# An adaLN attention and Mish block on one core: six weight slices split in the prologue, constant rows filled by GpSimd, loads respaced, and one TensorE visit for each modulation vector

## The chip, the cores and the metric

The kernel runs on one core of a Trainium2 chip. The time is what the device takes for one launch, in microseconds (us), taken as the median of several runs. The engines are TensorE (PE; its weight loads are PEld), VectorE (DVE), ScalarE (ACT), GpSimd (POOL) and SyncE (SP). All of the kernel's transfers are issued by SP, in one order, and run on the core's 16 DMA engines.

## The reference

A block of a transformer that is conditioned by a vector `c`, in float32, with 2048 rows of width 512, 32 heads of 16, and a hidden width of 1792:

```python
mod = (_silu(c) @ w_mod).reshape(c.shape[0], 6, 1, -1)
sa, ca, ga, sb, cb, gb = (mod[:, 0], mod[:, 1], mod[:, 2], mod[:, 3], mod[:, 4], mod[:, 5])
h = _layernorm(x, axis=-1) * (1 + ca) + sa
x = x + ga * _A_ref(h, A_wqkv, A_wo)          # softmax attention over all 2048 keys
h = _layernorm(x, axis=-1) * (1 + cb) + sb
x = x + gb * _B_ref(h, B_w1, B_b1, B_w2)      # (h @ w1 + b1) -> mish -> @ w2
```

The six modulation vectors are numbered 0 to 5 in this order, so `ga` is 2 and `gb` is 5.

## The kernel before

**Precision.** Products that must keep float32 accuracy are made from a high and a low part of each operand (`hi_copy`, L89, and `lo_sub`, L97): three products instead of one. Weights are split once and kept in DRAM as pairs (`w1scr`, `woscr`, `w2scr`).

**Steps.** Attention is worked in 32 turns `n`: a turn is four heads against one block of 512 queries, and has 16 steps `t`, so the main loop (`step`, L1227) has 512 steps. A step makes four 128x512 blocks of scores (L536), their exponentials on ACT (L539), the products with the values (`pv`, L554, once in a step), and, for the turn that comes 20 steps later, the row maxima of the scores (L487 on TensorE, L489 on VectorE). Scores, maxima and transposes share a ring of six PSUM banks. The maxima leave VectorE as a small tile `mt` (`max_rows`, L514), and SP writes it in four transfers of 4 KB into two extra rows of the query tiles `qa`, so that the score product subtracts the maximum itself. That put stands six half steps (three steps) before turn `n` starts, and must have landed by then.

**Work beside.** A score or maximum product uses 64 of TensorE's 128 rows. The other 64 rows take the remaining matrix products: the projections of q, k and v for later heads, the output product with `wo`, and the MLP. They wait in a list of units (`next_part`, L1185) that every two steps take up to eight products from, and small jobs stand in a list of specials (`do_specials`, L1330), which is visited after a step's products and goes to TensorE's queue between them and the step's `pv`.

**Order.** Nothing is scheduled by a compiler. The order is written out by hooks: `at(h, f)` runs `f` at half step `h = 2t`, and so places its instructions on the queue of each engine; a turn has 32 half steps. Half steps below 0 are the prologue, in which the maxima of turn 0 and part of turn 1 are made while the first projections run (`whole_units`, L1204). `store_at` (L193), `load_at` (L198) and `clear` (L189) move the stores and loads of the weight slices out of the half steps around the puts of `mt` (half step 26 of a turn). An engine's queue runs in order, so a hook's place does not tell its time: SP goes on as soon as the next transfer's buffer and data are free.

**Constant rows.** The key tiles `ka` and query tiles `qa` (five pairs in turn) have 64 rows for each of two heads: 48 rows of data, then rows of ones in `ka` and rows of zeros or of `mt` in `qa`. `zer` and `one` are 128x512 tiles; SP copies them into `qa` (`zeros`, L413) and into `ka` 0 and 1 (L419); `ka` 2 to 4 get their ones from `ka` 0 (L1428).

**Modulation.** Vectors 2 to 5 are each made in two halves: `mod_load` (L645) loads 512 KB of `w_mod`, three GpSimd operations multiply it by silu(c) and halve it twice (L652 to L654), and a special (`mod_unit`, L658) sums the 128 partitions on TensorE. For a gate (2 and 5) a half is one product of 256 columns, else two of one column.

**Weight slices.** 32 slices of 256 KB (14 of w1, 4 of wo, 14 of w2) are each loaded, split on GpSimd and stored as 512 KB (`prep_unit`, L678), one after the other by `start_preps` (L1392) from half step 60 on. Their tile `hl` has two buffers, later three. When all are stored and the projections are done, the memory of the projections becomes the MLP's (`prep_step`, L1403), and `first_loads` (L822) brings the first weights and rows of x.

```python
then = load_at(max(h + PREP, puts[0] + 1 if len(puts) > 2 - (not three) else 0))
at(then, lambda: start_preps(then, i + 1, turn + 1 if three else 0, puts))
```

Of the kernel before, what the change touches and what calls it, by code (L numbers as in the profile page):

```python
# [8 lines left out]
F32 = mybir.dt.float32  # L9
F32R = mybir.dt.float32r  # L10
# [8 lines left out]
def adaln_block(ctx: ExitStack, tc: tile.TileContext, x, wqkv, wo, w1, b1, w2, c, w_mod, out):  # L19
# [104 lines left out]
    def mm(acc, l, r, start, stop):  # L124
        pe_queue.append((acc, l, r, start, stop))
# [71 lines left out]

    def load_at(h):  # L198

        return h if h < 60 or 2 <= h % 32 < 20 else h - h % 32 + 28 if 20 <= h % 32 <= 28 else h + -(h - 2) % 32  # L200

    def at(h, f):

# [122 lines left out]
    with ExitStack() as es:  # L326
# [22 lines left out]
        slice_load(1, 1, pw)  # L349
        zer = lp.tile([P, TB], F32, name="zer")  # L350
        nc.gpsimd.memset(zer, 0.0)
        one = lp.tile([P, TB], F32, name="one")
        nc.gpsimd.memset(one, 1.0)

        e = lp.tile([P, DK], F32, name="sil_e")
        nc.scalar.activation(e, cc, AF.Exp, scale=-1.0)
# [53 lines left out]
        stats_tb(1)  # L410
        tr_tb(0)
        apply_tb(1)
        def zeros(i):  # L413
            for b in (48, 112):
                nc.sync.dma_start(qa[i][b:b + 16, :].bitcast(F32), zer[:16, :])

        for i in range(2):
            for b in (48, 112):
                nc.sync.dma_start(ka[i][b:b + 16, :].bitcast(F32), one[:64, :])  # L419
            zeros(i)  # L420

        def constants():
            for i in range(2, NR):
                zeros(i)
# [40 lines left out]

    kq2 = ctx.enter_context(tc.tile_pool(name="kq2", bufs=1))
    ka += [kq2.tile([P, S], F32R, name=f"ka{i}") for i in range(2, NR)]
    ap = ctx.enter_context(tc.tile_pool(name="ap", bufs=1, reuse_waits="tile"))
    vgs = {}

# [186 lines left out]

    def mod_unit(i):  # L658

        v, o = divmod(i, 2)  # L660
        gate = v in (2, 5)
        acc, row = ring(), mst.pop(("wm", i))[:, 0]
        if gate:
            mm(acc[:, :2 * P], ones.to_broadcast([P, P]), row, True, True)
        else:
            for m in range(2):
                mm(acc[:, m:m + 1], row[:, m * P:(m + 1) * P], ones, True, True)

        def fin(h):
            if gate:  # L670
                nc.scalar.copy(gates[(v - 2) // 3][:, o * 2 * P:(o + 1) * 2 * P], acc[:, :2 * P])
            elif v == 4:
                nc.vector.tensor_scalar_add(modc[:, v - 1, 2 * o:2 * o + 2], acc[:, :2], 1.0)
            else:
                nc.vector.tensor_copy(modc[:, v - 1, 2 * o:2 * o + 2], acc[:, :2])
        return fin

    def prep_unit(h, third, scr, src, gate):  # L678
# [113 lines left out]
    def block(qb, t0):  # L792
# [7 lines left out]
        def load(h, d, load_, keys):  # L800

            for j, k in enumerate(keys):
                at(h + 2 * j, lambda k=k: d.__setitem__(k, load_(k)))

        def more_w2(h, n):

            for j in range(n):
                k = mst["w2 at"]
                b, i = divmod(k, DK + FT)
                mst["w2 at"] += 1  # L810
                if b < NB - 1:
                    d, f, i = (state[b][3], load_wo, i) if i < DK else (state[b][2], load_w2, i - DK)
                    load(h + 2 * j, d, f, (i,))
                    if f is load_wo and i == DK - 1:
                        mst["wo at", b] = h + 2 * j
                elif i >= DK and i < DK + 3:
                    load(h + 2 * j, state[b][2], load_w2, (i - DK,))
                else:
                    mst["w2 at"] -= 1
                    break  # L820

        def first_loads(h):  # L822
            mst["w2 at"] = 0
            more_w2(h + 1, NA)
            load(h + 2, y, lambda i: load_y(qb, i), range(4))
            load(h + 9, w1s, load_w1, range(2))
            for i in range(4):
                mst["y at", qb, i] = h + 2 + 2 * i

# [529 lines left out]
        return fin  # L1359

    at(-2 * PRO, lambda: slice_load(*plan[2][1:3]))
    order = (4, 5, 10, 11, 6, 7, 8, 9)

    def first_mods(h):
        for i in order[:2]:
            mod_load(i, h)

    def queue_mod(j):
        def make():
            put = mod_unit(order[j])  # L1370

            def fin(h):
                put(h)
                if j + 2 < len(order):
                    mod_load(order[j + 2], h)
                elif j + 1 == len(order):
                    start_preps(h + 2)
            return fin

        queue_special(lambda: mst.get(("row at", order[j]), 4 * T) + 6, make)  # L1380

    for j in range(len(order)):
        queue_mod(j)
# [8 lines left out]
    def start_preps(h, i=0, turn=0, puts=()):  # L1392

        if i == len(preps):
            mst["open"] = (max(puts) + 2) // 2
            return
        three = (2, 1, NKC - 1) in put_away
        prep_unit(h, three and turn % 3 == 2, *preps[i])
        puts = (*puts, store_at(h + 9))[-3 if three else -2:]
        then = load_at(max(h + PREP, puts[0] + 1 if len(puts) > 2 - (not three) else 0))  # L1400
        at(then, lambda: start_preps(then, i + 1, turn + 1 if three else 0, puts))

    def prep_step(t):  # L1403
# [19 lines left out]
    at(2 * (T - 28), lambda: load_ys((0, 1)))  # L1423
    at(2 * (T - 12), lambda: load_ys((2,)))
    at(2 * T - 30, tail_loads)
    for pp in range(2, NR):
        for b in (48, 112):
            nc.sync.dma_start(ka[pp][b:b + 16, :].bitcast(F32), ka[0][b:b + 16, :].bitcast(F32))  # L1428
    for pp, h in ((2, -22), (3, -8)):
        at(h, lambda pp=pp: load_pair(pp))  # L1430
    def run_hooks(h):
# [39 lines left out]
```

## Time and profile before

| what | us |
|---|---|
| median of 3 runs (1700.04 to 1704.23) | 1703.48 |
| the profiled execution | 1704.48 |
| its span, first to last instruction | 1702.7 |
| start of the first `pv` (L554) | 109.7 |
| start of the last `pv` | 1600.8 |

The profile has a page of summaries; other views give single instructions in order of time (the timeline: start, duration, engine, line, what it writes and reads, how many, and in brackets the idle time before it with what ended it), the waits of each engine, and for chosen stretches the busy time of each engine, TensorE's granted clock (PEclk, 1.00 is full) and the share of time in which the 16 DMA engines were busy. A row of SP shows when a transfer is issued, not when it lands.

### The profile page before, as it was taken

What the parts mean: (1) busy time and instruction counts of PE and PEld (TensorE: products, weight loads), DVE (VectorE), ACT (ScalarE), POOL (GpSimd) and SP (SyncE); (2) the same over time, 40 slices, a digit from 0 to 9 for tenths busy, and PEclk for the clock granted to TensorE, in tenths of its full rate; (3) what the DMA queues carried; (4) which work ended last, traced back from release to release, by engine and by line L of the source; (5) the groups of instructions that cost most, each with busy time, mean ns of one, the idle gap of its engine ahead of it and who ended that gap; (6) DMA issues with size and microseconds to landing.
All of it is one profiled execution on the core that took longest, in us unless ns stands there. A gap on an engine that the chain in (4) does not pass through costs nothing.

```text
span 1702.7 us, 33730 instructions
## 1 busy us (share of the span) xinstructions
PE 1674.4 (98%) x12406; PEld 921.7 (54%) x12406; DVE 1438.2 (84%) x2372; ACT 1359.4 (80%) x2614; POOL 809.3 (48%) x829
## 2 busy tenths in 40 slices
PE   7999999999999999999999999999999999999999
PEld 5755665455444545555555455555555455555587
DVE  6888888888889898888889898888889888884377
ACT  6257777777778998888888998888888988888674
POOL 5155224565513465645433464655323564555442
PEclk9999999999999999999999999999999999999999
DMA  7777467777773343425364434435354433433261
GB/s 252 186 233 216 111 163 214 238 229 217 236 219 94 89 105 90 128 78 135 80 161 122 129 73 109 124 76 139 78 141 134 130 93 76 142 105 127 78 229 62
DMA packets 113997, 240.08 MB, mean 141 GB/s; under 512 B 24048, under 2 KB 49648, under 8 KB 107784
## 3 DMA queue, kind: packets, MB, share of 16 engines
q1 hardware_dynamic: 113832, 237.92, 49.5%
q8 instruction: 98, 1.61, 0.4%
q14 instruction: 67, 0.55, 0.1%
HBM read 179.95 MB, written 51.44 MB: 136 GB/s over the span
## 4 chain that ended last, share of the span: by engine, by line
PE 90%; DVE 3%; DMA 3%; ACT 2%; issue 1%; SPq 0%; POOL 0%; ACTq 0%; DVEq 0%; POOLq 0%
PE bk L554 28%; PE ring L536 22%; PE ring L487 19%; PE bk L136 10%; PE bk L129 3%; PE ring L1162 2%; PE ring L129 2%; DVE mx L489 2%; ACT pr L539 1%; DMA qa<-mt 1%; DMA xt<-in_A_x 1%; PE ring L501 1%; DMA w<-w1scr 1%; DMA w<-woscr 1%; PE ring L865 0%
## 5 line engine op out<-in xcount | busy, mean ns | idle before, releaser
L489 DVE TENSOR_REDUCE mx<-ring 128x1 f32<-128x512 f32 x1968 | 1222.9, 682 | 159.5 <-PE ring L487 138.0
L539 ACT ACTIVATE pr<-ring 128x512 f32<-128x512 f32 x2048 | 1079.0, 602 | 216.2 <-PE bk L136 118.0
L487 PE MATMUL ring<-ka,qa 64*128 64x512 f32 x1968 | 819.0, 429 | 3.0 <-DMA od<-ot 1.3
L536 PE MATMUL ring<-qa,ka 64*128 64x512 f32 x2048 | 761.3, 403 | 6.8 <-DMA qa<-mt 4.0
L554 PE MATMUL bk<-pr,vg 128*32 128x512 f32 x4096 | 546.8, 606 | 0.0
L487 PEld LDWEIGHTS ring<-ka,qa 64*128 64x128 f32 x1968 | 350.8, 184 | 331.6 <-DVE mx L489 248.1
L536 PEld LDWEIGHTS ring<-qa,ka 64*128 64x128 f32 x2048 | 374.1, 184 | 201.5 <-DVE mx L489 114.0
L136 PE MATMUL bk<-h,w 64*128 64x512 f32 (+1 forms) x1080 | 279.0, 391 | 0.0
L136 PE MATMUL bk<-w,a_h 64*128 64x512 f32 x632 | 210.6, 413 | 0.0
L136 PEld LDWEIGHTS bk<-h,w 64*128 64x128 f32 x1080 | 178.3, 184 | 9.6 <-ACT pr L539 1.5
L554 PEld LDWEIGHTS bk<-pr,vg 128*32 128x32 f32 x4096 | 80.8, 108 | 136.9 <-issue 127.8
L136 PE MATMUL bk<-w,a_l 64*128 64x512 f32 x316 | 124.2, 393 | 0.0
L136 PEld LDWEIGHTS bk<-w,a_h 64*128 64x128 f32 x632 | 106.9, 184 | 2.6
L921 POOL TENSOR_TENSOR y<-yd,y 128x512 f32<-128x512 f32 x44 | 56.9, 1293 | 89.5 <-ACT yd L920 84.6
L756 POOL TENSOR_SCALAR qq<-ee 128x512 f32<-128x512 f32 x25 | 15.5, 622 | 169.1 <-ACT ee L750 169.1
L772 POOL TENSOR_TENSOR qq<-qq,rr 128x512 f32<-128x512 f32 x42 | 54.2, 1291 | 83.6 <-ACT rr L766 83.4
L758 POOL TENSOR_TENSOR hb<-hb,ee 128x512 f32<-128x512 f32 x42 | 54.1, 1289 | 82.4 <-DVE ee L754 80.4
L136 PE MATMUL bk<-w,o_hl 64*128 64x512 f32 x288 | 79.8, 407 | 0.0
L98 POOL TENSOR_TENSOR a_l<-hb,a_h 128x512 fp32r<-128x512 f32 x53 | 72.2, 1363 | 4.4
L136 PEld LDWEIGHTS bk<-w,a_l 64*128 64x128 f32 x316 | 58.3, 184 | 2.3
L136 PE MATMUL bk<-h_h,wl 64*128 64x512 f32 x168 | 57.5, 423 | 0.0
L774 POOL TENSOR_TENSOR rr<-rr,qq 128x512 f32<-128x512 f32 x42 | 54.1, 1289 | 3.5
(206 smaller groups left out, 1857.9 us busy)
## 6 DMA issues: line engine op xcount, KB each, us to landing
ka<-kscr SPq DMA_DIRECT2D x124, 384.0 KB
w<-w2scr SPq DMA_DIRECT2D x56, 512.0 KB
w<-w1scr SPq DMA_DIRECT2D x46, 512.0 KB
vg<-vscr SPq DMA_DIRECT2D x32, 552.0 KB
qa<-qscr SPq DMA_DIRECT2D x124, 100.0 KB
kscr<-qh SPq DMA_DIRECT2D x16, 512.0 KB
qscr<-qh SPq DMA_DIRECT2D x32, 256.0 KB
hl<-in_B_w SPq DMA_DIRECT2D x28, 256.0 KB
```

Of the source, the lines that this page charges most:

```text
L98: (nc.gpsimd if eng == "p" else nc.vector).tensor_sub(lo, src, hi.bitcast(F32))
L129: nc.tensor.matmul(acc, l, r, start=start, stop=stop)
L136: i = nc.tensor.matmul(acc, l[64 * g:64 * g + 64], r[64 * g:64 * g + 64], start=start and not then, stop=bool(stop and then))
L487: nc.tensor.matmul(pm, qt[64 * s:64 * s + 64, qs * P:(qs + 1) * P], kt[64 * s:64 * s + 64, kb * TB:(kb + 1) * TB], start=True, stop=True)
L489: nc.vector.tensor_reduce(out=mxs[n][:, s, 4 * j + qs, kb:kb + 1], in_=pm, op=ALU.max, axis=AX.X)
L536: nc.tensor.matmul(p_, kt[64 * s:64 * s + 64, kc * P:(kc + 1) * P], qt[64 * s:64 * s + 64, :], start=True, stop=True)
L539: e = nc.scalar.activation(pr, p_, AF.Exp, scale=SCALE)
L554: nc.tensor.matmul(accs[n][32 * h:32 * h + 32, :], vgs[n][:, o:o + 32], pts.pop((t, h)), start=(kc == 0), stop=(kc == 15))
L758: (nc.vector if tail else nc.gpsimd).tensor_mul(hb, hb, ee)
L772: nc.gpsimd.tensor_mul(qq, qq, rr)
L774: nc.gpsimd.tensor_mul(rr, rr, qq)
L921: nc.gpsimd.tensor_add(y[i], yd, y[i])
```

## The change

```diff
-        return h if h < 60 or 2 <= h % 32 < 20 else h - h % 32 + 28 if 20 <= h % 32 <= 28 else h + -(h - 2) % 32
+        return h if h < 60 or 4 <= h % 32 < 20 else h - h % 32 + 28 if 20 <= h % 32 <= 28 else h + -(h - 4) % 32
...
-        one = lp.tile([P, TB], F32, name="one")
-        nc.gpsimd.memset(one, 1.0)
+        for i in range(NR):
+            nc.gpsimd.memset(qa[i].bitcast(F32), 0.0)
+        for i in range(2):
+            nc.gpsimd.memset(ka[i].bitcast(F32), 1.0)
...
-        def zeros(i):
-            for b in (48, 112):
-                nc.sync.dma_start(qa[i][b:b + 16, :].bitcast(F32), zer[:16, :])
-
-        for i in range(2):
-            for b in (48, 112):
-                nc.sync.dma_start(ka[i][b:b + 16, :].bitcast(F32), one[:64, :])
-            zeros(i)
...
+    for t in ka[2:]:
+        nc.gpsimd.memset(t.bitcast(F32), 1.0)
...
-    def mod_unit(i):
-
-        v, o = divmod(i, 2)
+    def mod_unit(v):
+
         gate = v in (2, 5)
-        acc, row = ring(), mst.pop(("wm", i))[:, 0]
-        if gate:
-            mm(acc[:, :2 * P], ones.to_broadcast([P, P]), row, True, True)
-        else:
-            for m in range(2):
-                mm(acc[:, m:m + 1], row[:, m * P:(m + 1) * P], ones, True, True)
+        acc, rows = ring(), [mst.pop(("wm", 2 * v + o))[:, 0] for o in range(2)]
+        for o, row in enumerate(rows):
+            if gate:
+                mm(acc[:, o * 2 * P:(o + 1) * 2 * P], ones.to_broadcast([P, P]), row, True, True)
+            else:
+                for m in range(2):
+                    mm(acc[:, 2 * o + m:2 * o + m + 1], row[:, m * P:(m + 1) * P], ones, True, True)
...
-            more_w2(h + 1, NA)
+            more_w2(h + 1, DK)
             load(h + 2, y, lambda i: load_y(qb, i), range(4))
-            load(h + 9, w1s, load_w1, range(2))
+            load(t0 + 7, w1s, load_w1, range(2))
+            at(t0 + 10, lambda: more_w2(t0 + 11, NA - DK))
...
-    order = (4, 5, 10, 11, 6, 7, 8, 9)
-
-    def first_mods(h):
-        for i in order[:2]:
-            mod_load(i, h)
+    order = (2, 5, 3, 4)
+
+    def first_mods(h, j=0):
+        for o in range(2):
+            mod_load(2 * order[j] + o, h + 2 * o)
...
+    EARLY = 6
+
+    def early_prep(i, h):
+
+        scr, src, _ = preps[i]
+        lo, hi = [ap.tile([P, TB], F32R, tag=f"p{(1, 3, 0, 2)[i % 4]}", name="ep", bufs=4 - i % 4 // 2) for _ in range(2)]
+        raw = lo.bitcast(F32)
+        nc.sync.dma_start(raw.rearrange("p (k m) -> p k m", m=P), src)
+
+        def split():
+            hi_copy("p", hi, raw)
+            lo_sub("p", lo, raw, hi)
+
+        def put():
+            for v, part in enumerate((hi, lo)):
+                nc.sync.dma_start(scr[:, v, :], part.bitcast(F32))
+
+        at(h + 7, split)
+        at(h + 10, put)
+
+    for i in range(EARLY):
+        at(3 * i - 34, lambda i=i: early_prep(i, 3 * i - 34))
...
-        then = load_at(max(h + PREP, puts[0] + 1 if len(puts) > 2 - (not three) else 0))
+        then = load_at(max(h + PREP, puts[0] + 2 if len(puts) > 2 - (not three) else 0))
...
-            at(32 * (n - 2) + (15 if n % 2 == 0 else 9), lambda n=n: load_pair(2 * n))
+            at(32 * (n - 2) + (2 if n in (3, 4, 5, 7) else 15 if n % 2 == 0 else 9), lambda n=n: load_pair(2 * n))
...
-    for pp in range(2, NR):
-        for b in (48, 112):
-            nc.sync.dma_start(ka[pp][b:b + 16, :].bitcast(F32), ka[0][b:b + 16, :].bitcast(F32))
```

The first six slices of w1 go through tiles of the exponentials' buffers during the prologue (`early_prep`), and `start_preps` begins with slice 6, at half step 66 instead of 60. The five `qa` and five `ka` tiles are filled whole by GpSimd. Both halves of a vector are loaded at one hook and their products stand in one special; the second half's three GpSimd operations come two half steps after the first's. The first pair of tiles of turns 3, 4, 5 and 7 is loaded 7 to 13 half steps earlier. Of the MLP's first loads, two slices of w1 and three of w2 come some 30 half steps later.

Three places on SP's queue show what moves. The first is the prologue, from the constants on; `ka` and `qa` with a number are the tiles of one pair, `wr` a raw slice of wqkv, `ep` a raw slice of w1, `vq` values on their way to DRAM. Before:

```order
L428 DMA b1c<-in_B_b 128x14x1
L1428 DMA ka_634<-ka_104 16x2048 x2
L1428 DMA ka_635<-ka_104 16x2048 x2
L1428 DMA ka_636<-ka_104 16x2048 x2
L231 DMA wr<-in_A_wqkv 128x4x128
L295 DMA vscr<-vq 128x4x272 x2
L310 DMA qa_108<-qscr 50x512 x2
L319 DMA ka_634<-kscr 48x2048 x2
```

and changed:

```order
L419 DMA b1c<-in_B_b 128x14x1
L231 DMA wr<-in_A_wqkv 128x4x128
L1393 DMA ep<-in_B_w 128x4x128 x2
L295 DMA vscr<-vq 128x4x272
L1393 DMA ep<-in_B_w 128x4x128 x2
L295 DMA vscr<-vq 128x4x272
L1401 DMA w1scr<-ep 128x512 x2
L1393 DMA ep<-in_B_w 128x4x128
L310 DMA qa_108<-qscr 50x512 x2
L319 DMA ka_625<-kscr 48x2048 x2
```

The six copies of ones are gone, and slice loads and their stores stand ahead of the next pair of tiles. The second place is the put of `mt` for turn 5 (`hl` is a slice, `rb` the reciprocal sums, `vg` the values). Before:

```order
L231 DMA wr<-in_A_wqkv 128x4x128
L689 DMA w1scr<-hl 128x1024
L682 DMA hl<-in_A_wo 128x512
L592 DMA rb<-rscr 64x1x512
L689 DMA woscr<-hl 128x1024
L474 DMA vg<-vscr 128x1104
L269 DMA qscr<-qh 8x16x512 x2
L269 DMA qscr<-ql 8x16x512
L525 DMA qa_106<-mt 2x4x128
```

and changed:

```order
L231 DMA wr<-in_A_wqkv 128x4x128
L675 DMA hl<-in_B_w 128x512
L682 DMA woscr<-hl 128x1024
L585 DMA rb<-rscr 64x1x512
L467 DMA vg<-vscr 128x1104
L269 DMA qscr<-qh 8x16x512 x2
L269 DMA qscr<-ql 8x16x512
L682 DMA woscr<-hl 128x1024
L518 DMA qa_106<-mt 2x4x128
```

The slice's load no longer stands behind the store just ahead of it, and one slice's store has moved from ahead of `vg` to right ahead of the four puts. The third place is the second pair of turn 9 (`qa_110`), behind the MLP's first loads (`y` are rows of x, `w` weight pairs). Before:

```order
L713 DMA y<-in_A_x 128x512
L695 DMA w_5841<-w2scr 128x1024
L695 DMA w_5843<-w1scr 128x1024
L695 DMA w_5869<-w2scr 128x1024
L695 DMA w_5871<-w1scr 128x1024
L310 DMA qa_110<-qscr 50x512 x2
L319 DMA ka_636<-kscr 48x2048 x2
```

and changed:

```order
L706 DMA y<-in_A_x 128x512
L688 DMA w_5833<-woscr 128x1024
L706 DMA y<-in_A_x 128x512
L310 DMA qa_110<-qscr 50x512 x2
L319 DMA ka_627<-kscr 48x2048 x2
```

Four slices of 512 KB that stood between the rows of x and the pair have gone from there; one slice and one row tile have come in their place.

More of the change, by code (lines that the diff above doesn't have):

```diff
@@ L412, in adaln_block @@
         apply_tb(1)
-        def zeros(i):
-            for b in (48, 112):
-                nc.sync.dma_start(qa[i][b:b + 16, :].bitcast(F32), zer[:16, :])
-        for i in range(2):
-            for b in (48, 112):
-                nc.sync.dma_start(ka[i][b:b + 16, :].bitcast(F32), one[:64, :])
-            zeros(i)
         def constants():
-            for i in range(2, NR):
-                zeros(i)
             for q4 in range(S // TB):
@@ L656, in mod_load @@
         at(h + 7, sums)
-    def mod_unit(i):
-        v, o = divmod(i, 2)
+    def mod_unit(v):
         gate = v in (2, 5)
-        acc, row = ring(), mst.pop(("wm", i))[:, 0]
-        if gate:
-            mm(acc[:, :2 * P], ones.to_broadcast([P, P]), row, True, True)
-        else:
-            for m in range(2):
-                mm(acc[:, m:m + 1], row[:, m * P:(m + 1) * P], ones, True, True)
+        acc, rows = ring(), [mst.pop(("wm", 2 * v + o))[:, 0] for o in range(2)]
[5 more added lines that the diff above has]
+                    mm(acc[:, 2 * o + m:2 * o + m + 1], row[:, m * P:(m + 1) * P], ones, True, True)
         def fin(h):
             if gate:
-                nc.scalar.copy(gates[(v - 2) // 3][:, o * 2 * P:(o + 1) * 2 * P], acc[:, :2 * P])
+                nc.scalar.copy(gates[(v - 2) // 3], acc)
             elif v == 4:
-                nc.vector.tensor_scalar_add(modc[:, v - 1, 2 * o:2 * o + 2], acc[:, :2], 1.0)
+                nc.vector.tensor_scalar_add(modc[:, v - 1, :], acc[:, :DK], 1.0)
             else:
-                nc.vector.tensor_copy(modc[:, v - 1, 2 * o:2 * o + 2], acc[:, :2])
+                nc.vector.tensor_copy(modc[:, v - 1, :], acc[:, :DK])
         return fin
@@ L1373, in fin @@
                 put(h)
-                if j + 2 < len(order):
-                    mod_load(order[j + 2], h)
-                elif j + 1 == len(order):
+                if j + 1 < len(order):
+                    first_mods(h, j + 1)
+                else:
                     start_preps(h + 2)
             return fin
-        queue_special(lambda: mst.get(("row at", order[j]), 4 * T) + 6, make)
+        queue_special(lambda: mst.get(("row at", 2 * order[j] + 1), 4 * T) + 6, make)
     for j in range(len(order)):
@@ L1390, in adaln_block, with start_preps @@
     preps += [(w2scr[f], w2[f * P:(f + 1) * P, :], 1) for f in range(FT)]
-    def start_preps(h, i=0, turn=0, puts=()):
+    EARLY = 6
[14 more added lines that the diff above has]
+        at(3 * i - 34, lambda i=i: early_prep(i, 3 * i - 34))
+    def start_preps(h, i=EARLY, turn=0, puts=()):
         if i == len(preps):
```

## Prediction, made before the changed kernel was run

> **What bounds the kernel now.** I read the page first: its busy times, the chain of waits, then the groups that the chain waits in.
>
> ```profile
> PE 1674.4 (98%) x12406; PEld 921.7 (54%) x12406; DVE 1438.2 (84%) x2372; ACT 1359.4 (80%) x2614; POOL 809.3 (48%) x829
> PE 90%; DVE 3%; DMA 3%; ACT 2%; issue 1%; SPq 0%; POOL 0%; ACTq 0%; DVEq 0%; POOLq 0%
> PE ring L536 <- DMA qa<-mt: 4.0, 3, 2.0
> PE ring L487 <- DMA od<-ot: 1.3, 1, 1.3
> ```
>
> PE is busy 98% of the span and 90% of the chain, so a transfer or a GpSimd operation counts only where PE waits for it. The view of waits (total, times, longest) has two such places in the main loop: three waits for the rows of `mt`, and one that it puts down to an output store. The timeline shows what they cost. A `pv` (L554) closes each step, so the distance of two `pv` is the step.
>
> ```profile
> 334.38 1.06 PE L554 MATMUL bk<-pr,vg 128*32 128x512 f32 x8
> 337.27 1.06 PE L554 MATMUL bk<-pr,vg 128*32 128x512 f32 x8
> 340.32 0.46 PE L536 MATMUL ring<-qa,ka 64*128 64x512 f32 x1 [1.98 <-DMA qa<-mt]
> 342.76 1.08 PE L554 MATMUL bk<-pr,vg 128*32 128x512 f32 x4
> ...
> 435.84 0.46 PE L536 MATMUL ring<-qa,ka 64*128 64x512 f32 x1 [1.76 <-DMA qa<-mt]
> ...
> 490.74 1.06 PE L554 MATMUL bk<-pr,vg 128*32 128x512 f32 x8
> 494.03 0.46 PE L487 MATMUL ring<-ka,qa 64*128 64x512 f32 x1 [1.26 <-DMA od<-ot]
> 496.12 1.94 PE L554 MATMUL bk<-pr,vg 128*32 128x512 f32 x8
> 500.04 1.06 PE L554 MATMUL bk<-pr,vg 128*32 128x512 f32 x8
> ```
>
> A step takes 337.27 - 334.38 = 2.89. The first step of turn 5 takes 342.76 - 337.27 = 5.49, and the two steps around 494 take 500.04 - 490.74 = 9.30 instead of 5.78: 3.52 lost for a gap of 1.26. The granted clock tells why (window, length, busy time of PE, PEld, DVE, ACT and POOL, PEclk, DMA share, GB/s):
>
> ```profile
> 341.00:346.00 5.00, 5.00 (x32) 2.29 (x29) 3.13 (x6) 2.60 (x6) 3.88 (x5) 0.66 0.94 190
> 494.00:498.00 4.00, 3.97 (x22) 1.57 (x22) 2.09 (x4) 1.77 (x3) 0.00 (x0) 0.62 0.06 11
> ```
>
> Behind both gaps the clock falls to 0.66 and 0.62 of full. At 0.66 over 5.00 us the loss is 0.34 x 5.00 = 1.70, so turn 5 costs about 1.98 + 1.60 = 3.58. For turn 7 I count the gap alone, 1.76.
>
> **What makes the puts late.** SP's rows and the DVE rows that make `mt`:
>
> ```profile
> 320.13 0.50 SPq L689 DMA_DIRECT2D w1scr<-hl  x1
> 327.86 0.33 SPq L682 DMA_DIRECT2D hl<-in_A_wo  x1
> 330.05 0.34 DVE L519 SCALAR_TENSOR_TENSOR mt<-mh,lows,ring 32x128 fp32r<-32x128 f32 x1 [0.42 <-ACT mh L518]
> 332.85 2.76 SPq L525 DMA_DIRECT2D qa<-mt  x4
> ...
> 379.68 0.34 DVE L519 SCALAR_TENSOR_TENSOR mt<-mh,lows,ring 32x128 fp32r<-32x128 f32 x1 [0.41 <-ACT mh L518]
> 380.10 2.77 SPq L525 DMA_DIRECT2D qa<-mt  x4
> ...
> 428.46 2.97 SPq L525 DMA_DIRECT2D qa<-mt  x4
> ...
> 477.48 0.33 SPq L695 DMA_DIRECT2D w<-w2scr  x1
> 481.12 0.80 SPq L319 DMA_DIRECT2D ka<-kscr  x2
> ```
>
> At turn 5 `mt` is ready at 330.39, but its first put goes out at 332.85, 2.46 later. SP stood 7.2 us between the store at 320.13 and the load at 327.86, which needs the store's buffer back; the rest of the queue follows. At turn 6 (380.02 to 380.10) SP is in time, and no wait is named. At turn 9 the pair is issued at 481.12 behind four weight slices of 512 KB, 12.9 us before PE goes on at 494.03; that the wait is for this pair and not for the store `od` is my reading, since the waiting product reads `ka` and `qa` only.
>
> **The change, part by part.**
>
> *Respaced slices* (load two half steps behind the store, not one). SP is no longer held, so the puts go out when `mt` is ready: 2.46 earlier at turn 5, more than the wait of 1.98. But the order shows a slice's store right ahead of the puts at turns 5 to 7. The rows that price transfers, and that serve the prologue too:
>
> ```profile
> 60.00:64.00 4.00, 4.00 (x30) 3.06 (x29) 3.41 (x4) 0.75 (x2) 0.00 (x0) 1.00 0.34 97
> 64.00:72.00 8.00, 8.00 (x59) 6.46 (x57) 7.09 (x7) 1.50 (x4) 0.00 (x0) 1.00 0.52 84
> 72.00:76.00 4.00, 4.00 (x31) 3.48 (x30) 3.73 (x4) 0.37 (x1) 0.00 (x0) 1.00 1.00 176
> 89.00:91.00 2.00, 2.00 (x11) 1.15 (x10) 1.68 (x3) 0.32 (x1) 0.00 (x0) 1.00 1.05 399
> 98.00:103.00 5.00, 4.73 (x22) 3.09 (x22) 5.00 (x5) 1.21 (x2) 2.52 (x3) 1.00 0.77 266
> 188.00:190.00 2.00, 1.93 (x24) 1.75 (x20) 1.84 (x4) 1.87 (x4) 0.00 (x0) 1.00 0.86 235
> ```
>
> At the 399 GB/s of 89:91, where only stores ran, 512 KB take 1.31. If that stands wholly ahead, the puts gain 2.46 - 1.31 = 1.15, and 0.83 of wait stays at turn 5, about as much at turn 7: 0 to 1.6 in all. I take 0.8. Terms: -3.58, -1.76, +0.8.
>
> *First loads respaced.* Four slices leave the place ahead of the pair at 481; one slice and one row tile, 0.75 MB, come. The net 1.25 MB take 3.3 at 399 and 5.6 at the 235 GB/s of 188:190, both above the wait of 1.26. Term: -3.52. The loads that go behind are issued some 15 steps later, long before the products that read them by their place in the code; if they were late, PE would wait there instead, and I bound that by the 3.52 that goes here.
>
> *Pairs loaded earlier, preparations from half step 66.* Both move transfers where no PE wait is named: 0.
>
> *One visit for both halves.* A gate's visit before:
>
> ```profile
> 118.51 1.06 PE L554 MATMUL bk<-pr,vg 128*32 128x512 f32 x8
> 121.48 0.67 PE L129 MATMUL ring<-wm,ones 128*128 128x256 f32 x2
> 122.08 1.06 PE L554 MATMUL bk<-pr,vg 128*32 128x512 f32 x8
> ```
>
> The step takes 3.57, so 0.68 more than 2.89, nearly the length of its products (0.67). Eight visits cost at most 8 x 0.68 = 5.4. Four remain, with the same number of products, so what goes is the change between them: 0 if the products are all of it, half of 5.4 if the visit is. Against it, the visit waits for the second half's GpSimd operations, which can have a split of 0.62 + 1.29 (rows below) ahead of them on POOL; I bound this by the longer of the two, +1.3. From -2.7 to +1.3, I take -0.4, nearer to the products.
>
> *Constants by GpSimd.* At the head POOL fills five `qa` and two `ka`:
>
> ```profile
> 2.34 0.59 POOL L351 MEMSET zer<- 128x512 f32 x1
> 13.08 0.20 POOL L371 TENSOR_SCALAR ln_rs<-ln_mv 128x4 f32<-128x4 f32 x1 [9.68 <-DVE ln_mv L370]
> ```
>
> 512 columns take 0.59, so 2048 take an estimated 2.36: 5 x 0.59 + 2 x 2.36 = 7.7, inside the 9.68 that POOL idles until 13.08. Cost 0; without that cover, up to 7.7. The three later `ka` are 7.1 more, in the prologue; there, of SP, POOL and PE:
>
> ```profile
> 60.17 3.73 SPq L415 DMA_DIRECT2D qa<-zer  x6
> 70.81 3.80 SPq L1428 DMA_DIRECT2D ka<-ka  x6
> 79.83 1.29 POOL L98 TENSOR_TENSOR wl<-wr,wh 128x512 fp32r<-128x512 f32 x1 [27.05 <-ACT wh L91]
> 91.78 0.62 POOL L95 TENSOR_SCALAR qh<-qf 128x512 fp32r<-128x512 f32 x1 [4.85 <-DMA kscr<-qh]
> 102.95 0.47 PE L536 MATMUL ring<-qa,ka 64*128 64x512 f32 x1 [0.27 <-DMA qa<-mt]
> ```
>
> POOL idles 27.05 before 79.83. The splits of the six slices, 6 x (0.62 + 1.29) = 11.5, then share POOL with the projections' splits; the row at 91.78 shows 4.85 in hand.
>
> *Six slices in the prologue.* This is the price of the change. It ends at 102.95, where the first score already waits 0.27 for `mt`: no slack. DMA gets six loads of 256 KB (1.12 each at 235) and six stores of 512 KB (1.31 each): 14.6. It loses the copies of ones, six of 128 KB, 0.79 MB at the 176 GB/s of 72:76: 4.5. Room without delay is what idles in 64:72, 0.48 x 8 = 3.8, in 98:103, 0.23 x 5 = 1.15, and, since SP sheds the 3.73 + 3.80 of issue, in 60:64, 0.66 x 4 = 2.6. So 14.6 - 4.5 - 3.8 - 1.15 - 2.6 = 2.5, or 5.1 without the last; none of the room in front used gives 14.6 - 4.5 - 1.15 = 9.0; all of it beside other work would give -0.3 at best. A gap's slow clock could add 1.6. I take +2.5: SP's earlier start is certain by the order.
>
> Sum: -3.58 - 1.76 + 0.8 - 3.52 - 0.4 + 2.5 = -6.0. The profiled execution took 1704.48 (span 1702.7), so it becomes 1698.5; it stood 1.0 above the median of 1703.48, so the median becomes 1697.5.
>
> **The rivals.**
>
> *The prologue takes all back.* The slices' transfers find no room in front, and `mt` for turn 0 comes 9.0 later: -6.0 + 6.5 = +0.5, 1704. For it: 72:76 and 89:91 are full. Against: 64:72 is half empty and SP comes there sooner.
>
> *The store ahead of the puts.* Slower: the puts at turns 5, 6 and 7 wait behind a 512 KB store. The old gaps stay, as the DMA engines are what holds, and grow by 1.31; turn 6, in time by 0.08 at SP, gets 1.31 plus a slow clock of 1.6, turn 7 the same, turn 5 only 1.31: +7.1. With -3.52 - 0.4 + 2.5 that is +5.7: 1709. It decides once the store lands later than `mt` plus what turn 6 has in hand, which no row shows. For it: 341:346 has DMA at 0.94. Against: that store's buffer and the values come some 7 us earlier than before.
>
> *Only the gaps return.* If the slow clock did not come from the gap, it would stay where it is: -1.98 - 1.76 - 1.26 + 0.8 - 0.4 + 2.5 = -2.1, 1701. Against it: both drops stand right behind a gap, and turns without one have none that I found.
>
> The Trainium skill has a rule that would make this so (TensorE: Matmul & The Clock Gate, What's actually happening): the clock halves after at least one idle window of about 3.4 us. The trace disagrees: gaps of 1.98 and 1.26 were followed by 0.66 and 0.62.
>
> **How the numbers follow.** A measurement of this kernel can tell about 0.3%, 5.1 us, from no change: faster is below 1698.4, slower above 1708.6. Forecast 0.58, its own range 1692 (-8.9 - 2.7 - 0.3 = -11.9) to 1704 (prologue 5.1 + 1.6, visits +1.3, 1.6 of wait left: +0.7); being so near the bound it gives faster 0.46 and same 0.12. Prologue takes all: 0.14, same 0.11, slower 0.03 with the slow clock on top. Gaps alone: 0.05, same. Store ahead of the puts: 0.23, slower 0.20, same 0.03. Together: faster 0.46, same 0.31, slower 0.23. The range runs from 1692 to 1711, the slower rival with the prologue at 5.1 (1709 + 2.6, cut at 1711), and leaves out some 0.15.
>
> **What would show it.** In the profile after, PE's waits for `qa<-mt` at turns 5 and 7 and for `od<-ot` near 494 should be gone or below 0.9, and the `pv` there 2.9 apart with PEclk 1.00. The first `pv` should come some 2.5 later. The first score's wait for `mt` should rise from 0.27 by what the slices delay; if it rises by 9, the first rival holds. POOL's splits should not stand right before a late `qh`. A wait at turn 6 shows the slower rival. The forecast is wrong above all if the prologue's transfers are not served in the room that I count, or if the visits wait for the second half.

## The result, and the profile after

| | before | changed |
|---|---|---|
| median of 22 runs | 1701.78 | 1699.13 |
| all runs | 1698.25 to 1704.89 | 1697.36 to 1701.20 |
| ratio, with its 95% interval | | 0.9982 (0.9977 to 0.9988) |
| the profiled execution | 1704.48 | 1697.49 |
| its span | 1702.7 | 1695.7 |

The change makes the kernel 2.65 us faster by the medians, inside the stated range and on the forecast's side, but less than half of the 6.0 forecast. The prediction called a kernel faster only below 1698.4, so by its own words this is "same", to which it gave 0.31, and not "faster", to which it gave 0.46. Its range, 1692 to 1711, holds the time of before too, so that the result fell inside says little. The two profiled executions, though, lie 7.0 apart. The profile of before stands 2.7 above its median, that of the change 1.6 below. That difference is the main thing that the experiments had to explain.

The page after, in the rows that answer to those shown of before (busy times, the chain), and two rows of its groups (what they do, count, busy time and mean ns, idle time ahead and its releaser):

```profile
PE 1672.8 (99%) x12406; PEld 924.7 (55%) x12406; DVE 1437.8 (85%) x2370; ACT 1358.3 (80%) x2612; POOL 820.1 (48%) x838
PE 91%; DVE 4%; ACT 2%; DMA 2%; issue 0%; SPq 0%; POOL 0%; ACTq 0%; DVEq 0%
L480 PE MATMUL ring<-ka,qa 64*128 64x512 f32 x1968 | 818.8, 430 | 1.6 <-ACT pr L532 1.1
L529 PE MATMUL ring<-qa,ka 64*128 64x512 f32 x2048 | 760.8, 403 | 5.4 <-DMA qa<-mt 2.6
```

PE's waits for the rows of `mt` fall from 4.0 to 2.6, and no maxima product (L480) waits for a transfer any more. The timeline of PE shows where the 2.6 lie, and the places of before:

```profile
105.40 0.47 PE L529 MATMUL ring<-qa,ka 64*128 64x512 f32 x1 [1.96 <-DMA qa<-mt]
...
336.22 1.06 PE L547 MATMUL bk<-pr,vg 128*32 128x512 f32 x8
339.12 1.06 PE L547 MATMUL bk<-pr,vg 128*32 128x512 f32 x8
341.96 1.06 PE L547 MATMUL bk<-pr,vg 128*32 128x512 f32 x8
...
433.00 0.46 PE L529 MATMUL ring<-qa,ka 64*128 64x512 f32 x1 [0.59 <-DMA qa<-mt]
...
487.95 1.07 PE L547 MATMUL bk<-pr,vg 128*32 128x512 f32 x8
490.80 1.06 PE L547 MATMUL bk<-pr,vg 128*32 128x512 f32 x8
493.69 1.06 PE L547 MATMUL bk<-pr,vg 128*32 128x512 f32 x8
```

Turn 5 starts at 340.1 without a stall (2.90 and 2.84 between its `pv`), turn 7 keeps 0.59, and the pair of turn 9 costs nothing (2.85 and 2.89). The first score of all, though, now waits 1.96 for `mt` instead of 0.27. The SP rows of turn 0, GpSimd's rows ahead of them, and the SP rows of turn 7 say why:

```profile
99.53 0.38 SPq L231 DMA_DIRECT2D wr<-in_A_wqkv  x1
99.96 0.50 SPq L273 DMA_DIRECT2D kscr<-qh  x1
100.51 0.46 SPq L274 DMA_DIRECT2D kscr<-ql  x1
101.08 2.96 SPq L518 DMA_DIRECT2D qa<-mt  x4
...
96.98 1.27 POOL L98 TENSOR_TENSOR ql<-qf,qh 128x512 fp32r<-128x512 f32 x1 [0.92 <-DMA kscr<-ql]
98.21 1.28 POOL L98 TENSOR_TENSOR wl<-wr,wh 128x512 fp32r<-128x512 f32 x1
...
424.61 1.49 SPq L682 DMA_DIRECT2D w2scr<-hl  x1
426.21 3.02 SPq L518 DMA_DIRECT2D qa<-mt  x4
```

At turn 0 the puts go out at 101.08, 1.55 later than in the kernel before. They stand behind the load of a raw slice `wr`, which goes out when GpSimd has read the buffer that it needs: at 99.49, in the kernel before at 97.95. GpSimd had itself waited 0.92 for a store of `kscr` to land; in the kernel before it does not wait there. At turn 7 a slice's store, 1.49 of SP's time, stands right ahead of them.

The start of the first and of the last `pv` cuts an execution in three. For all profiles of this study, in us; ratios are to the kernel before, run beside it; "one run" has no ratio:

| kernel | first pv | first to last pv | behind the last pv | span | median | ratio (95%) |
|---|---|---|---|---|---|---|
| before | 109.7 | 1491.1 | 102.0 | 1702.7 | 1701.78 | |
| before_again | 110.8 | 1486.5 | 102.0 | 1699.3 | 1701.99 | 0.9996 (0.9987 to 1.0005) |
| before_third | 110.4 | 1488.5 | 102.0 | 1700.8 | one run | |
| the change | 112.4 | 1481.6 | 101.7 | 1695.7 | 1699.13 | 0.9982 (0.9977 to 0.9988) |
| after_again | 112.1 | 1482.4 | 101.7 | 1696.3 | 1698.45 | 0.9982 (0.9969 to 0.9995) |
| first_loads_only | 109.8 | 1487.5 | 102.4 | 1699.6 | 1702.22 | 0.9999 (0.9988 to 1.0010) |
| slices_only | 110.4 | 1485.2 | 126.0 | 1721.6 | 1722.20 | 1.0117 (1.0101 to 1.0133) |
| no_early | 109.6 | 1483.1 | 131.2 | 1723.8 | 1726.50 | 1.0140 (1.0125 to 1.0156) |
| early1 | 109.8 | 1485.3 | 125.0 | 1720.2 | one run | |
| early3 | 111.0 | 1485.5 | 117.8 | 1714.3 | 1715.16 | 1.0066 (1.0048 to 1.0084) |
| early3_puts | 109.9 | 1485.8 | 114.3 | 1710.0 | 1714.60 | 1.0068 (1.0051 to 1.0086) |
| put_first | 111.6 | 1482.2 | 101.7 | 1695.5 | 1697.95 | 0.9984 (0.9976 to 0.9993) |
| store_late | 112.1 | 1482.1 | 101.7 | 1696.0 | 1698.31 | 0.9981 (0.9971 to 0.9990) |
| two_visits | 112.3 | 1483.1 | 101.7 | 1697.1 | one run | |

### The profile page after: what moved, and what is told of

Read it like the earlier page. It is cut to its first block, busy times and chain, and to the rows that moved or that the text cites. A ratio compares the mean times of both kernels' runs of the same rounds, so it can differ in the third digit from the quotient of the medians.

```text
span 1695.7 us, 33728 instructions
## 1 busy us (share of the span) xinstructions
PE 1672.8 (99%) x12406; PEld 924.7 (55%) x12406; DVE 1437.8 (85%) x2370; ACT 1358.3 (80%) x2612; POOL 820.1 (48%) x838
## 4 chain that ended last, share of the span: by engine, by line
PE 91%; DVE 4%; ACT 2%; DMA 2%; issue 0%; SPq 0%; POOL 0%; ACTq 0%; DVEq 0%
PE bk L547 29%; PE ring L529 23%; PE ring L480 20%; PE bk L136 9%; PE bk L129 3%; PE ring L1156 2%; DVE mx L482 2%; PE ring L129 2%; ACT pr L532 1%; DMA xt<-in_A_x 1%; PE ring L494 1%; DMA qa<-mt 1%; PE ring L859 0%; PE ring L509 0%; DVE hf L392 0%
## 5 line engine op out<-in xcount | busy, mean ns | idle before, releaser
L480 PE MATMUL ring<-ka,qa 64*128 64x512 f32 x1968 | 818.8, 430 | 1.6 <-ACT pr L532 1.1
L480 PEld LDWEIGHTS ring<-ka,qa 64*128 64x128 f32 x1968 | 351.2, 184 | 327.8 <-DVE mx L482 251.0
L95 POOL TENSOR_SCALAR qh<-qf 128x512 fp32r<-128x512 f32 x27 | 16.8, 622 | 82.8 <-ACT qf L259 56.3
```

The lines of the kernel that those rows point to most:

```text
L480: nc.tensor.matmul(pm, qt[64 * s:64 * s + 64, qs * P:(qs + 1) * P], kt[64 * s:64 * s + 64, kb * TB:(kb + 1) * TB], start=True, stop=True)
```

## The experiments

### The kernels again: do the waits repeat?

No edit; the kernel before twice more, the change once more.

> The kernel before, unchanged, to see how far its profile repeats. The profiled execution stood 2.7 us above the median of 22 runs (1701.78), that of the change 1.6 below its own (1699.13), so 4.3 of the 7.0 us between the two profiles are not in the medians. Theory A (the three waits are fixed by the queue, what varies is the clock behind them): the gaps at the first score of turn 5, of turn 7 and at the second pair of turn 9 come again within 0.3 us of 1.98, 1.76 and 1.26, and the span differs through the granted clock. Theory B (the waits themselves vary): one of the gaps is missing or more than 1 us different. Ratio to the kernel before 1.000 within 0.001 in both.

> The kernel before once more, for a third look at its waits. If the three waits of the first profile (5.0 us of gaps, 8.9 with the slow clock) were typical, their sum recurs within 2; by the medians (main loop typically about 4.6 longer than that of the change, 1.1 of it the visits) the gaps of turns 5 to 8 and of the second pair of turn 9 with their slow clock are 3.5 in the typical run, so this profile's main loop lies at 1485 to 1489 and not at 1491.

> The changed kernel once more. Theory B' (which waits fall in an execution varies, and the change removes most of them but lengthens the prologue): first pv again near 112.4 (111.5 to 113), no gap over 1 us after the first score, main loop (first to last pv) within 1.5 of 1481.6 against 1486 to 1491 in the two profiles of the kernel before; ratio to the kernel before 0.998 to 0.999. Rival (the profile of the change was a lucky one): a gap of 1.5 or more at one of turns 5 to 8 and a main loop above 1484.

The first gaps of turns 5, 6 and 7 and of turn 9's second pair, beside how long after `mt` was ready SP issued the first put (from the rows of DVE and SP), in us:

| profile | turn 5: late, gap | turn 6: late, gap | turn 7: late, gap | pair of turn 9: gap |
|---|---|---|---|---|
| before | 2.46, 1.98 | 0.08, none | 2.33, 1.76 | 1.26 |
| before_again | 0.14, none | 2.35, 1.67 | 0.44, none | 0.73 |
| before_third | 1.48, 0.90 | 2.03, none | 2.57, 1.73 | 1.42 |
| the change | 0.06, none | 0.41, none | 1.75, 0.59 | none |
| after_again | 0.06, none | 0.06, 0.97 | 0.06, none | none |

Theory A falls: which turn stalls differs between executions of one kernel. The mechanism holds all the same: in the kernel before the put is late where SP stood behind a slice's load, and it hits turns 5 and 7 in one execution and turn 6 in the next. PE in before_again:

```profile
384.56 1.06 PE L554 MATMUL bk<-pr,vg 128*32 128x512 f32 x8
387.29 0.61 PE L536 MATMUL ring<-qa,ka 64*128 64x512 f32 x1 [1.67 <-DMA qa<-mt]
390.45 1.25 PE L554 MATMUL bk<-pr,vg 128*32 128x512 f32 x8
```

This step takes 5.89, 3.0 over its usual 2.88. SP in the same profile, with the slice's load at 375.15 behind an idle stretch of 4.7 (SP's last row ended at 370.43), and the put 2.35 after `mt` (377.67):

```profile
369.57 0.38 SPq L590 DMA_DIRECT2D rscr<-rc  x1
370.05 0.38 SPq L689 DMA_DIRECT2D w2scr<-hl  x1
375.15 0.33 SPq L682 DMA_DIRECT2D hl<-in_B_w  x1
...
380.02 3.02 SPq L525 DMA_DIRECT2D qa<-mt  x4
```

The change's second profile has one gap of 0.97 at turn 6 though its first put was in time. There no slice's load holds SP: two of the four puts wait for earlier transfers to land (0.4 for `rb`, 0.7 for `vg`), and the four take 3.87, against 2.77 in the first profile. That this makes the gap is read from the rows and not tested. The gap stayed below the 1.5 that the rival named. before_third came at 1488.5, inside 1485 to 1489; its gaps add up to 4.1 (5.0 in the first profile), with the slow clock to 6.5 (8.9).

The wait of turn 9 is, in before_third, put down to the pair's own load, as I had read it against the name in the first profile:

```profile
489.03 1.06 PE L554 MATMUL bk<-pr,vg 128*32 128x512 f32 x8
492.54 0.55 PE L487 MATMUL ring<-ka,qa 64*128 64x512 f32 x1 [1.42 <-DMA ka<-kscr]
495.21 1.53 PE L554 MATMUL bk<-pr,vg 128*32 128x512 f32 x8
498.58 1.06 PE L554 MATMUL bk<-pr,vg 128*32 128x512 f32 x8
```

Means over the profiles (three of before, two of the change): first `pv` 110.3 against 112.3, first to last `pv` 1488.7 against 1482.0. So the change costs 2.0 in the prologue, wins 6.7 in the main loop and 0.2 behind it, 4.9 in all by so few profiles; the medians of 22 runs say 2.65, with an interval of 2.0 to 3.9.

### First loads alone

```diff
-            more_w2(h + 1, NA)
+            more_w2(h + 1, DK)
             load(h + 2, y, lambda i: load_y(qb, i), range(4))
-            load(h + 9, w1s, load_w1, range(2))
+            load(t0 + 7, w1s, load_w1, range(2))
+            at(t0 + 10, lambda: more_w2(t0 + 11, NA - DK))
```

> The kernel before with only the MLP's first loads respaced. Theory A: the gap of 1.26 at the second pair of turn 9 is gone with the slow clock behind it, 3.5 us less, ratio 0.998; first pv at 109.7 and the gaps of turns 5 and 7 as before. Theory B: the gap is gone too, but the typical run had little of it, so the ratio is 0.9993 or more. If the wait was for the output store that the profile names and not for the pair's load, the gap stays at about 1.3.

The gap at the pair of turn 9 is gone, so the cause is right. But the ratio is 0.9999, and this profile has gaps of 2.50 at turn 7 and 1.45 at turn 8. Theory B holds for the time: no gain is visible, and the interval allows at most 2.0 us. Whether those two gaps are luck or follow from the edit one profile can't say; up to the opening at t=121 the two programs have the same transfers in the same order, and turn 7 lies before it.

### Slices respaced alone

```diff
-        return h if h < 60 or 2 <= h % 32 < 20 else h - h % 32 + 28 if 20 <= h % 32 <= 28 else h + -(h - 2) % 32
+        return h if h < 60 or 4 <= h % 32 < 20 else h - h % 32 + 28 if 20 <= h % 32 <= 28 else h + -(h - 4) % 32
...
-        then = load_at(max(h + PREP, puts[0] + 1 if len(puts) > 2 - (not three) else 0))
+        then = load_at(max(h + PREP, puts[0] + 2 if len(puts) > 2 - (not three) else 0))
```

> The kernel before with only the slices respaced (a slice's load two half steps behind the store, not one), so the MLP's memory opens later as well. Theory A: gaps at turns 5 and 7 below 0.9 each; the first loads come later and miss the second pair of turn 9, so that its gap goes too: main loop 8 to 9 us shorter than in the first profile, ratio 0.996 to 0.997 against typical runs. Rival (the store that now stands right ahead of the puts takes the place of the wait): gaps of 1.3 to 3 at turns 5, 6 and 7, ratio 1.002 to 1.004. Second rival: the late opening pushes the MLP's work to the end, and the last pv is no earlier or what follows it is longer by more than 1.

The waits of turns 5 to 7 are gone, as theory A said: puts 0.06, 0.06 and 0.36 after `mt`, no gap over 0.5 at turns 5 to 8. All profiles together say the same: each of the four with the old spacing (the kernel before three times, first_loads_only) has a gap of 1.67 or more there, the ten with the new spacing have none above 0.97. The wait at turn 9's pair is gone too, but one of 1.02 for the next turn's pair has come at 532.96, behind the later first loads. The rival of the store ahead of the puts falls as a loss: it is there and costs little. But the kernel is 20 us slower, which the second rival foresaw, and far more than its 1 us. Each slice now takes longer, the 32 are done later, and the MLP's memory opens at step t=138 of the main loop instead of 121. PE behind the last `pv`:

```profile
1603.18 0.62 PE L129 MATMUL bk<-w,a_h 128*128 128x512 f32 x2
1603.64 0.40 PE L129 MATMUL bk<-w,a_l 128*128 128x512 f32 x1
1614.71 1.22 PE L129 MATMUL bk<-w,a_h 128*128 128x512 f32 x2 [10.67 <-POOL a_h L95]
```

Products of the MLP that used to run beside scores run here alone, and the last of them wait 10.67 for `a_h`, the high part of the MLP's hidden values, from GpSimd. The end is 24 longer (126.0 against 102.0).

### Without the early slices, and with fewer

Six early slices become none, one or three. In no_early the first loads are those of before as well, since the opening comes too late for the others.

```diff
-    EARLY = 6
+    EARLY = 0
```

> The changed kernel without the six early slices (all 32 from half step 66), with the first loads as before, since they now come after the opening of the MLP's memory. Theory A: the prologue's extra is the early slices': first pv back to 109.7 from 112.4, the wait of the first score for mt back to 0.3 from 1.96, gaps of turns 5, 7 and 9 still gone, so some 2.7 below the changed kernel, ratio to the kernel before 0.9966. Rival: GpSimd's constants are what costs in the prologue: first pv stays within 0.7 of 112.4. Second rival: the early slices are needed: the memory opens at t=140 instead of 122, and the end is longer, so the ratio is 0.998 or more.

> The changed kernel with one early slice; the memory opens at t=138, as in slices_only, whose end was 24 us longer. Theory A'': first pv at 109.7 to 110.3; the end is longer by 20 to 30, as the first loads miss the first units. If the end stays near 101.7, the longer end of slices_only and no_early came from the place of their first loads and not from the opening.

> The changed kernel with three early slices instead of six; the memory of the MLP opens at t=132 instead of 122. Theory A'' (the slices in the prologue cost by their number; the opening costs only when the first weights and rows come too late for the first unit, which no step before about 136 does): first pv near 111, halfway from 109.6 (none) to 112.3 (six), what follows the last pv stays near 101.7, main loop 1481.5 to 1484; 1 below the changed kernel, ratio to the kernel before 0.9975. Rival (every step of later opening is paid at the end): 10 steps later give, with 24 to 29 us for openings at 138 to 140 against none at 122, some 13 to 15 us more behind the last pv, ratio above 1.004.

| early slices | first pv | opening at t | behind the last pv |
|---|---|---|---|
| 0 (no_early) | 109.6 | 140 | 131.2 |
| 1 | 109.8 | 138 | 125.0 |
| 3 | 111.0 | 132 | 117.8 |
| 6 (the change) | 112.4 | 122 | 101.7 |

Two readings. The prologue's extra comes from the slices and not from GpSimd's constants: with all constants on GpSimd and no slice, the first `pv` stands at 109.6, where it stood before, and no PE wait is named at the first score. And the slices are needed: without them the kernel is slower by a ratio of 1.0140, as the second rival said. early1 has the change's first loads and ends as late as slices_only, so the end goes by the opening and not by the place of those loads. My theory that an opening up to about step 136 is free was wrong at three slices, where the rival was right (13 to 15 foreseen, 16.1 measured); its main loop, 1485.5, is above what I expected as well. From 122 to 132 the end grows by 1.6 for each step of later opening.

### The puts first, the store late

```diff
-        at(2 * (16 * n + 16 - PRO) + 2, put)
+        put()
```

and for store_late and early3_puts (this one with three early slices) besides:

```diff
-        return h if h < 60 or h % 32 < 22 else h - h % 32 + 27
+        return h if h < 60 or h % 32 < 21 else h - h % 32 + 27
```

> The changed kernel with the four puts of mt ahead of the other transfers of their half step on SP's queue; this moves them for turn 0 (ahead of a raw slice of wqkv and two stores of k) and, as to waits, nowhere else. If the prologue's extra is the puts' place on SP behind what GpSimd delivers late: the first put goes out within 0.5 of mt (96.5 instead of 101.08), the first score waits less than 0.3 instead of 1.96, its slow clock (0.80 in 105 to 110) is gone, first pv near 109 instead of 112.4, 3 below the changed kernel: ratio to the kernel before 0.996 to 0.997. If it is the DMA engines, full with the slices, that hold the puts: the first score waits still over 1, first pv at 111 or later. Third possibility: k and q that now come behind the puts are late for turn 1, and the time lost comes back within the first 32 steps.

> put_first, and the slice's store that stood right ahead of the puts at turns 5 to 7 put off until behind them. If that store is what holds the puts of turn 7 (1.75 after mt, a gap of 0.59): first put within 0.1 of mt at turns 5, 6 and 7 and no gap over 0.2 there; 0.5 below put_first, within what can be told. If the DMA engines' backlog holds them, a gap of about 0.6 stays at one of these turns.

> Three early slices, the puts ahead of the other transfers of their half step, and the slices' stores put off until behind the puts. With the end at 101.7: first pv 110 to 111, no gap above 0.3 at turns 5 to 8, main loop 1481 to 1483, so 1 to 2 below the changed kernel and ratio 0.997 to the kernel before. If the opening at t=132 costs, the end is longer by over 5.

In put_first the first put of turn 0 goes out at 96.23, 0.15 after `mt`, and the first score starts at 102.67 without a wait. Three scores later PE stops all the same. PE, and then ACT in the same stretch:

```profile
102.67 0.50 PE L529 MATMUL ring<-qa,ka 64*128 64x512 f32 x1
...
105.89 0.50 PE L529 MATMUL ring<-qa,ka 64*128 64x512 f32 x1 [2.25 <-ACT pr L532]
...
97.34 0.59 ACT L259 COPY qf<-bk 128x512 f32<-128x512 f32 x1 [2.26 <-POOL ql L98]
104.09 0.62 ACT L91 CAST wh<-wr 128x512 fp32r<-128x512 f32 x1 [6.16 <-DMA wr<-in_A_wqkv]
104.75 0.59 ACT L259 COPY qf<-bk 128x512 f32<-128x512 f32 x1
105.23 4.04 ACT L532 ACTIVATE pr<-ring 128x512 f32<-128x512 f32 x8
```

The exponentials stand behind the cast of a raw slice of wqkv, whose load was issued behind the puts now. The wait has only moved from `mt` to `wr`: the first `pv` comes 0.8 earlier, not 3, and store_late, with the same order of the puts, has 112.1, so even the 0.8 is within the scatter. What all of it seems to wait for is the DMA engines. Windows of the change, then of before_again:

```profile
60.00:72.00 12.00, 12.00 (x89) 9.87 (x89) 10.82 (x10) 2.20 (x7) 5.52 (x4) 1.00 0.92 227
88.00:92.00 4.00, 4.00 (x19) 2.56 (x20) 3.30 (x4) 0.59 (x1) 1.57 (x3) 1.00 1.06 402
92.00:96.00 4.00, 4.00 (x20) 2.54 (x18) 3.97 (x6) 1.26 (x3) 2.41 (x3) 1.00 1.07 404
```

```profile
60.00:72.00 12.00, 12.00 (x88) 9.56 (x86) 10.49 (x10) 2.25 (x6) 0.00 (x0) 1.00 0.48 96
88.00:92.00 4.00, 4.00 (x19) 2.68 (x18) 3.61 (x4) 0.59 (x1) 0.00 (x0) 1.00 1.10 365
92.00:96.00 4.00, 4.00 (x22) 2.51 (x20) 3.97 (x6) 1.27 (x3) 2.83 (x4) 1.00 1.05 278
```

The idle half of 60 to 72 is used up (share 0.92 against 0.48). From 88 to 96 the engines have no time left in either kernel (shares 1.05 to 1.10), and the change has more to move there, 400 GB/s against 365 and 278. In no_early, the change without the slices, the shares from 88 to 96 are 0.69 and 0.82, so the slices are what fills the engines in the change. That the full engines are what delays `wr` and the puts fits these rows, but no run tests it apart from the slices.

In store_late the puts of turns 5 to 7 go out 0.06 to 0.07 after `mt`, and there is no gap at turns 5 to 8, as foreseen for the store; put_first had none either, so its profile can't tell the half microsecond, nor can the medians (1697.95 and 1698.31). early3_puts fails by its opening, as early3 did. None of these beats the change beyond what can be told.

### Two visits

```diff
-    def mod_unit(v):
+    def mod_unit(i):
...
-    order = (2, 5, 3, 4)
+    order = (4, 5, 10, 11, 6, 7, 8, 9)
```

> The changed kernel with each half of a modulation vector in a visit of its own again. The eight visits took 0.6 to 1.0 us each over a step of 2.88 in the kernel before, 5.6 together; the four of the change 1.04 to 1.12, 4.4 together. So the step list of turns 0 and 1 gains 1.1 to 1.3 us, and the rest is as in the changed kernel. Rival (the second half's GpSimd sums hold a joint visit): the separate visits show the same 0.6 to 0.7 each but a joint one would show PE waiting for GpSimd, which the first profile of the change doesn't.

PE of two_visits around a gate's first visits, then of the change:

```profile
121.17 1.06 PE L547 MATMUL bk<-pr,vg 128*32 128x512 f32 x8
124.13 0.67 PE L129 MATMUL ring<-wm,ones 128*128 128x256 f32 x2
124.73 1.06 PE L547 MATMUL bk<-pr,vg 128*32 128x512 f32 x8
127.69 0.67 PE L129 MATMUL ring<-wm,ones 128*128 128x256 f32 x2
128.29 1.06 PE L547 MATMUL bk<-pr,vg 128*32 128x512 f32 x8
```

```profile
124.08 1.06 PE L547 MATMUL bk<-pr,vg 128*32 128x512 f32 x8
127.04 1.10 PE L129 MATMUL ring<-wm,ones 128*128 128x256 f32 x4
128.07 1.07 PE L547 MATMUL bk<-pr,vg 128*32 128x512 f32 x8
```

Two visits make two steps of 3.56, 0.68 each over 2.88; the joint visit makes one of 3.99, 1.11 over. Over all vectors the excess is 5.5 against 4.3, so the joint visits save 1.2. No wait for GpSimd is named at the joint visits of either profile of the change. But the rival is not gone: with joint visits too, PE waits for the second half's sums at the first gate's visit 0.67 in early1, 0.28 in early3_puts and 0.29 in store_late, and that step is 2.05, 1.66 and 1.67 over.

## Why the prediction was right, and where it was not

**The puts of turns 5 and 7.** Forecast -3.58, -1.76 and +0.8 for what stays, together -4.5. In the two profiles that it was worked out for, the steps there got shorter by 3.55 and 1.11, together 4.7. (For turn 5 the working finds 1.70 for the slow clock and then adds 1.60; the rows have 1.57.) The mechanism (SP behind a slice's load that waits for its buffer) is shown by slices_only, where the puts are in time. What failed is the step ahead of the sum: it took the waits of one profiled execution for those of every execution. In the three profiles of before, the steps of turns 5 to 7 lost 5.3, 3.0 and 2.7 to these waits, 3.7 on the mean, and in the change's two 0.6 and 1.0; that gives -2.9. The +0.8 met its size by luck: what stayed is at turns 7 and 6, and none at turn 5, where 0.83 was reckoned.

**The pair of turn 9.** Forecast -3.52; -3.85 between the first two profiles, but 3.6, 0.9 and 3.8 in the three of before, 2.8 on the mean, and none in the change. The cause is shown (the gap goes in first_loads_only), its size was that of one execution. Even the mean may be too much: first_loads_only allows at most 2.0 for the edit, unless the edit costs something elsewhere, as its gap of 1.45 at turn 8 would.

**The visits.** Forecast -0.4, measured -1.2: the term was mis-sized. I chose the end where the products are all of the cost, since they last 0.67 and the step loses 0.68. But four products that stand together take 1.10, not twice the 0.67 of two, and the step loses 1.11, not 1.36.

**The prologue.** Forecast +2.5 (between -0.3 and 9.0); 2.7 between the first two profiles, 2.0 between the means. The room in 60 to 72 was used nearly as reckoned (0.44 of 12 us is 5.3, of the 6.4 that was counted), and the constants cost nothing, also as reckoned: three memsets of 2048 columns stand there on GpSimd, and no_early has its first `pv` at 109.6.

**A step that was missing.** I set the preparations from half step 66 and the respacing of the slices at nothing beyond the waits. Alone the respacing costs 20 us, through the opening of the MLP's memory at 138 instead of 121, and the six early slices buy that back (122). The two cancel in the change, so the sum did not suffer, but the prediction gave no reason for the slices, only their price. The pairs that are loaded earlier, set at nothing as well, no run took out alone; slices_only, which lacks them, already has no wait at turns 5 to 7.

**The total.** The means of the profiles give -2.9 - 2.8 - 1.2 + 2.0 = -4.9, the medians -2.65 (interval -3.9 to -2.0). The conversion from the profiled execution to the median, 1.0 by three runs, was 2.7 by 22: part of the stalls in the sum were that execution's own. The 2.3 between -4.9 and the medians are a matter of which executions were profiled. A run's time is 1.8 more than its span; the three spans of before lie on the mean 0.9 above that of its median run, and the change's two lie 1.0 to 1.6 below that of its own (1699.13 less 1.8). So there are executions of the change that wait more than those shown, and which of the terms shrinks in the typical run stays open.

**The rivals.** The prologue did not take all back. The store ahead of the puts is seen once, 0.59 at turn 7, not 7.1. That only the gaps return is refuted in the profiles: turn 5 gave back 3.55 for a gap of 1.98. Its sum of -2.1 is nearer to the medians' -2.65 than the forecast is, but by its number alone.

## What to carry to other kernels

A wait that hangs on when a buffer's store lands is not a fixed quantity: before a stall is put into a sum, look at several executions, and give it the mean and not what one profile shows. Respacing work that ends in a deadline (here the opening of the MLP's memory) moves the deadline; what pays for that has to stand in the sum even if it cancels. And where an engine's queue waits in a row for several late things, taking the first away shows the next, so follow the row to what it all waits for, here, as far as the windows show, full DMA engines.

## What the runs showed of the hardware

The slow clock behind a gap does not go by the gap's length. The granted clock in the 4 us from each gap's end, in before_again (gap 1.67), then in before_third (gap 1.73, and 1.42), then in first_loads_only (gap 2.50, and 1.45):

```profile
387.30:391.30 4.00, 4.00 (x22) 2.50 (x22) 2.60 (x4) 2.39 (x4) 1.83 (x2) 0.57 0.93 221
```

```profile
434.10:438.10 4.00, 4.00 (x32) 2.43 (x34) 3.15 (x6) 2.44 (x5) 3.14 (x4) 1.00 0.94 200
492.60:496.60 4.00, 4.00 (x20) 2.00 (x20) 2.23 (x4) 1.79 (x3) 0.00 (x0) 0.57 0.05 13
```

```profile
433.70:437.70 4.00, 4.00 (x32) 2.45 (x34) 3.14 (x6) 2.45 (x5) 2.51 (x3) 1.00 0.90 193
479.60:483.60 4.00, 4.00 (x32) 2.47 (x34) 3.17 (x6) 2.46 (x5) 0.00 (x0) 1.00 0.79 158
```

Gaps of 1.67 and 1.42 were followed by 0.57, gaps of 1.73, 2.50 and 1.45 by full speed. With the first profile's 1.98 and 1.26 (both slow) and 1.76 (full), a gap of 1.3 to 2.5 in the main loop costs either its length alone or 1.3 to 2.4 more, and nothing in these profiles says beforehand which. The Trainium skill (TensorE: Matmul & The Clock Gate, What's actually happening) describes a free-running window of about 3.4 us. That where in such a window a gap falls decides would fit this mixture, but no run here shows the window, and the slow stretches came after gaps shorter than it.
